# Clustered attention and two expert layers on one core: first pair's cluster steps by head, centroids loaded by ScalarE, more declared waits, new listed priorities

## The chip, the cores and the metric

The kernel runs on one core of a Trainium2 chip. The metric is the device time of one execution in microseconds (us), as the median of several runs. Beside it stands one profiled execution, with a trace of every instruction on TensorE (PE, with its weight loads PEld), VectorE (DVE), ScalarE (ACT), GpSimd (POOL) and SyncE (SP), which issues most DMAs.

## The reference, cut to what matters

```python
def _attn_ref(q, k, v, centroids):            # (2, 8, 768, 64) each; centroids (8, 16, 64)
    q_assign = argmax(einsum('bhsd,hcd->bhsc', q_n, c_n))   # all normalised
    k_assign = argmax(einsum('bhsd,hcd->bhsc', k_n, c_n))
    mask = q_assign[..., :, None] == k_assign[..., None, :]
    scores = where(mask, scale * q @ k.T, -1e9)
    attn = softmax(scores)
    return attn @ v
...
def _moe_ref(x, w_in, w_out):                 # 1536 x 512, 512 x 2048, 2048 x 512
    h = x @ w_in
    return (h * sigmoid(1.702 * h)) @ w_out
...
def _moe2_ref(x, w_in, w_out, g_ln):          # 512 x 1024, 1024 x 512
    ln = layer_norm(h * softmax(h)) * g_ln    # h = x @ w_in
    return ln @ w_out
```

Attention feeds the first layer, the first layer the second. In the attention a token sees only the tokens of its own cluster.

## The kernel before, in words

**The attention.** Sixteen heads (two batches of eight) go through in eight pairs. For a pair p, `operands_of` loads q and k, turns them on TensorE (`turn`, L557), splits each into a high and a low half (`turn_high` on ScalarE, L564 and L566; `turn_low` on VectorE, L573) and multiplies them with the centroids (`logits`, L587). The logits are copied (`logits_copy`, L594), turned back (`logits_turn`, L600), and five VectorE steps make a one-hot row of the first largest cluster: `cluster_max`, `cluster_equal`, `cluster_weigh`, `cluster_first` and `cluster_halves` (L608 to L631). The one-hot rows are turned (`cluster_turn`, L639), copied to SBUF (`cluster_copy`, L661) and moved by DMA into the operands `OP1` (`place_cluster`, through `move`, L664). For head 0 alone TensorE writes the rows without a DMA (`cluster_rows`, L647, and `cluster_place`, L655 and L657). Pairs 0 and 1 share the start: the whole of pair 0's loads and pair 1's come first.

For a head u, `peaks_of` multiplies nine tiles to find the largest score of each row (`peak`, L936, tile `sm`; `peak_max`, a VectorE reduction, L947, into `nma`). From these come the minimum (`peak_all`, L959), its transpose (`peak_turn`, L963) and a row of the operands (`peak_rows`, L968 on VectorE for the first two heads; later `peak_copy` and a DMA). `scores_of` multiplies the nine score tiles again with that row included (`score`, L995 and L996, tile `st` or `tx`), takes the exponential (L1004, ScalarE), casts to 16 bits (`cast`, L1009), takes the rest (`rest`, L1013, on GpSimd, or on VectorE where the tile "stays" in PSUM) and multiplies with the values (`value`, L1028 to L1032, tile `av`).

**Scales.** `values` bounds the values; `power_from` (L147 to L155) makes powers of two out of sums; `x_power` (L852, L853) makes the scale of the attention's result out of the longest value row (`longest`, L839). VectorE runs it.

**The layers.** `rest_of_layer` multiplies the first layer's hidden units (`Hidden.products`, L1200, tile `hps`), the second half of the program, from about 220 us, the rest (L1517, L1551, L1696). A second planner orders that half, and the diff does not touch it.

**What sets the order.** Every operation is a task of `Plan`, with a cost per engine, a due time, the tasks it comes after (`after`), and the buffer it takes or frees. `Plan.order` walks through a model of the engines, and at each step gives an engine the task with the lowest due time among those that are possible about then. A task with `shared=True` waits on VectorE until the modelled GpSimd is free. The order that comes out is the order in which each engine's queue is filled, and it is fixed when the kernel is built. Semaphores keep the true dependences. `SHIFTS` is a table of task numbers whose due times are shifted by fixed amounts. Where TensorE's modelled queue is empty in the first 36 us, dummy products are put in (L1339, tile `idle`).

```python
t = min((t["due"] - (STAY if eng == "PE" and t["kind"] and kind else 0.0), t["id"], i) for i, (a, t) in enumerate(at) if a <= first + ...)
```

Of the kernel before, what the change touches and what calls it, by code (L numbers as in the profile page):

```python
# [21 lines left out]
def kernel(  # L22
# [51 lines left out]
    XDUE = 30  # L74
    VDUE = 15
    VLC = dict(DVE=0.93, POOL=2.55)
    SOON = 10
    WAHEAD = -80
# [15 lines left out]
    ADUE = 4.5  # L94
    AVC = 0.373
    STAY = 0.0
# [71 lines left out]
    class Weight:  # L168
# [319 lines left out]
    t0 = add(dict(SP=(0.47, 0.18)), -70, lambda t: nc.sync.dma_start(cen, centroids.rearrange("h c d -> (h c) d")))  # L488
# [114 lines left out]
    def groups(t):  # L603
        return t.rearrange("p (g o) -> p g o", o=1).to_broadcast([P, G, C])

    def cluster_max(t, p):
        mxs[p] = oh_p.tile([P, G], F32, tag="mx", name="mx")
        nc.vector.tensor_reduce(out=mxs[p], in_=t["tile"], op=ALU.max, axis=AX.X)  # L608

    def cluster_equal(t, p):  # L610


        eqs[p] = t["tile"]
        nc.vector.tensor_tensor(out=eqs[p], in0=t["tile"], in1=groups(mxs[p]), op=ALU.is_equal)

    def cluster_weigh(p):
        nc.vector.tensor_tensor(
            out=eqs[p], in0=eqs[p], in1=first.rearrange("p (o c) -> p o c", o=1).to_broadcast([P, G, C]), op=ALU.mult
        )

    def cluster_first(p):
        m2s[p] = oh_p.tile([P, G], F32, tag="m2", name="m2")
        nc.vector.tensor_reduce(out=m2s[p], in_=eqs[p], op=ALU.max, axis=AX.X)

    def cluster_halves(p):

        eq = eqs.pop(p).rearrange("p (j s i) c -> p s j i c", s=2, i=2)
        m2 = m2s.pop(p).rearrange("p (j s i o) -> p s j i o", s=2, i=2, o=1)
        ohs[p] = oh_p.tile([P, NJ, 2, 2, C], BF16, tag="oh", name="oh")
        for s, op in enumerate((ALU.is_lt, ALU.is_equal)):  # L630
            nc.vector.tensor_tensor(  # L631
                out=ohs[p][:, :, s], in0=eq[:, s], in1=m2[:, s].to_broadcast([P, NJ, 2, C]), op=op
            )
# [54 lines left out]

    def operands_of(p):
# [4 lines left out]
        for s in range(2):  # L694
# [7 lines left out]
            for i in range(2):  # L702
                T["L", p, s, i] = add(
                    dict(SP=(0.65, 1.0)), n0 + LDUE if p > 1 else -62, lambda t, s=s, i=i: load(p, s, i),
                    after=[at("TT", p - 1, 2)] + late(True) if p > 1 else [],
                )
        for e in range(3):
# [4 lines left out]
                after=[a, at("ST", 2 * (p - NHL) + 1, NU - 1)],  # L712
# [5 lines left out]
        for n in range(2):  # L718
# [10 lines left out]
        b = add(dict(DVE=0.47), n0 + 18, lambda t, a=a: cluster_max(a, p), after=[a, at("C4", p - 1)])  # L729
        b = add(dict(DVE=0.47), n0 + 18, lambda t, a=a: cluster_equal(a, p), after=[b])  # L730
        b = add(dict(DVE=0.47), n0 + 19, lambda t: cluster_weigh(p), after=[b])
        b = add(dict(DVE=0.47), n0 + 20, lambda t: cluster_first(p), after=[b])
        b = T["C4", p] = add(
            dict(DVE=0.54), n0 + 21, lambda t: cluster_halves(p), after=[b, at("TO", p - 1)], frees=a
        )
        for e in range(0 if p else 3):
            a = add(dict(PE=0.3), n0 + 21, lambda t, e=e: cluster_rows(t, e), after=[b], take="ex")
# [4 lines left out]
        a = T["TO", p] = add(dict(PE=0.45), n0 + 22, lambda t: cluster_turn(t, p), after=[b], take="ex")  # L742
# [4 lines left out]
        for i in range(2):  # L747
            u = 2 * (p - NS) + i
            before = [at("ST", u, NU - 1), at("SM", u, NU - 1)]
# [58 lines left out]
    def values():  # L808
# [50 lines left out]
        add(dict(DVE=1.1), XDUE, lambda t, a=a: x_power(a), after=[a, scales["v"]], frees=a)  # L859
        T["VF"] = add(dict(DVE=0.1), 8, lambda t: factor(), after=list(scales.values()))  # L860
# [211 lines left out]
    def peaks_of(u):  # L1072
# [21 lines left out]
        if u >= RWS:  # L1094
# [9 lines left out]
            T["RW", u] = add(dict(SP=(0.65, 0.05)), n0 + NU - 18, lambda t: peak_row(u), after=[a, at("ST", u - 4, NU - 1)])  # L1104
# [3 lines left out]
    def scores_of(u):  # L1108
# [45 lines left out]
        if i:  # L1154
            a = add(
                dict(ACT=0.73, DVE=0.5), n + 12, lambda t: x_high(t, p), after=[T["N", u], T["N", u - 1], at("TX", p - 1, 0)],
# [3 lines left out]
            for e, c in enumerate((a, b)):  # L1160
                T["TX", p, e] = add(
                    dict(SP=(1.25, 0.9)), n + 20, lambda t, e=e: x_turn(p, e),
# [144 lines left out]
    for p in range(NH // 2):  # L1307
# [743 lines left out]
```

## Time and profile before

| what | value |
|---|---|
| median of 3 runs | 591.79 us (591.66 to 591.95) |
| the profiled execution | 592.09 us |
| its span in the trace | 590.3 us |
| PE busy | 579.9 us (98%) |
| DVE busy | 454.1 us (77%) |
| ACT busy | 418.5 us (71%) |
| POOL busy | 278.7 us (47%) |
| chain that ended last | PE 92%, DVE 4%, ACT 1%, DMA 1%, issue 1% |

The profiled execution lies 0.30 us above the median; 1.8 us of it lie outside the span. Busy shares are means over stages with different limits: the attention (to about 220 us) is one stage, the layers are another. Times in the trace count from the start of the span.

### The profile page before, as it was taken

Reading aid. Unit: us, or ns where it says so; the run is one execution under the profiler, and the core shown is the slowest. Engines: PE = TensorE matmul, PEld = TensorE weight load, DVE = VectorE, ACT = ScalarE, POOL = GpSimd, SP = SyncE. Lnnn points to the kernel's source line nnn. Section 1 sums busy time; section 2 is a strip of 40 time slices with the busy share of each in tenths; the row PEclk is TensorE's granted clock in tenths of the full one; section 3 lists DMA queues with packets and bytes.
Section 4 is the critical chain, followed back from the end, with each engine's and each line's share of the span. In section 5 each row is a group of like instructions: output and inputs, shape, how many; then the busy total and the mean of one; then the engine's idle time right before and its main releaser. Section 6 shows DMA issues by size and latency. Waiting matters only on the chain.

```text
span 590.3 us, 12602 instructions
## 1 busy us (share of the span) xinstructions
PE 579.9 (98%) x4790; PEld 387.1 (66%) x4790; DVE 454.1 (77%) x924; ACT 418.5 (71%) x799; POOL 278.7 (47%) x262
## 2 busy tenths in 40 slices
PE   7999999999999999999999999999999999999997
PEld 5788888888888876666666666666655664444444
DVE  5999998898999997899888731984996427996820
ACT  5799989988999978788878356563647614647831
POOL 7469979977778764344682037802100300133100
PEclk9999999999999999999999999999999999999999
DMA  8976969797773026443650530320000530043571
GB/s 206 229 190 151 218 136 204 154 193 154 152 146 63 17 64 203 146 140 145 213 180 1 179 109 0 108 72 0 1 2 1 72 72 0 37 72 82 113 146 53
DMA packets 79732, 65.28 MB, mean 111 GB/s; under 512 B 63620, under 2 KB 66520, under 8 KB 79672
## 3 DMA queue, kind: packets, MB, share of 16 engines
q1 hardware_dynamic: 79672, 64.49, 45.2%
q8 instruction: 37, 0.61, 0.4%
q14 instruction: 23, 0.19, 0.1%
HBM read 34.64 MB, written 3.15 MB: 64 GB/s over the span
## 4 chain that ended last, share of the span: by engine, by line
PE 92%; DVE 4%; ACT 1%; DMA 1%; issue 1%; SPq 0%; DVEq 0%; ACTq 0%
PE bank L1696 20%; PE hps L1200 16%; PE bank L1517 16%; PE st L995 6%; PE sm L936 5%; PE bank L1200 5%; PE bank L1551 5%; PE st L996 5%; PE av L1028 3%; PE av L1032 3%; PE ex L587 3%; PE av L1031 3%; PE ex L557 1%; DVE nma L947 1%; DMA reg<-in_q_dram 1%
## 5 line engine op out<-in xcount | busy, mean ns | idle before, releaser
L1013 POOL TENSOR_TENSOR ph<-p,ph 128x512 f16<-128x512 f32 x116 | 135.8, 1194 | 31.9 <-ACT ph L1009 17.8
L1200 PEld LDWEIGHTS <-reg 128*128 128x128 f16 x768 | 75.1, 98 | 48.9
L947 DVE TENSOR_REDUCE nma<-sm 128x1 f32<-128x512 f32 (+1 forms) x144 | 95.7, 681 | 5.7 <-PE sm L936 5.3
L1517 PE MATMUL bank<-g,reg 128*128 128x384 f16 x576 | 94.4, 326 | 0.0
L1200 PE MATMUL hps<-xT,reg 128*128 128x384 f16 x576 | 94.3, 326 | 0.0
L1517 PEld LDWEIGHTS <-reg 128*128 128x128 f16 x576 | 56.4, 98 | 37.2
L1215 POOL TENSOR_SCALAR g<-g,scl 128x384 f32<-128x384 f32 x40 | 37.4, 935 | 82.5 <-ACT g L1210 78.6
L1696 PE MATMUL bank<-reg,g 128*128 128x512 f16 (+1 forms) x366 | 75.0, 365 | 0.0
L1696 PEld LDWEIGHTS <-g 128*128 128x128 f16 x438 | 42.9, 98 | 46.8
L1004 ACT ACTIVATE p<-st 128x512 f32<-128x512 f32 x115 | 67.8, 601 | 7.8 <-PE st L996 5.0
L1009 ACT CAST ph<-p 128x512 f16<-128x512 f32 x107 | 64.2, 623 | 1.9 <-PE av L1032 1.2
L996 PE MATMUL st<-OP 97*128 97x512 f32 (+3 forms) x196 | 62.9, 336 | 0.0
L1028 PE MATMUL av<-vh,ph 128*128 128x65 f16 x576 | 62.2, 194 | 0.0
L1032 PE MATMUL av<-vh,ph 128*128 128x65 f16 x576 | 61.3, 195 | 0.7 <-DVE ph L1013 0.7
L1031 PE MATMUL av<-vh,ph 128*128 128x64 f16 x576 | 61.4, 193 | 0.0
L1028 PEld LDWEIGHTS <-ph 128*128 128x128 f16 x576 | 52.7, 99 | 11.0 <-issue 9.3
L936 PE MATMUL sm<-OP 80*128 80x512 f32 (+1 forms) x192 | 56.0, 359 | 1.7 <-DVE nma L947 1.4
L1032 PEld LDWEIGHTS <-ph 128*128 128x128 f16 x576 | 53.7, 97 | 1.0 <-DVE ph L1013 0.9
L1031 PEld LDWEIGHTS <-ph 128*128 128x128 f16 x576 | 53.8, 97 | 0.1
L1899 POOL TENSOR_TENSOR small<-small,mhalf 128x2 f32<-128x2 f32 (+1 forms) x7 | 4.6, 655 | 81.0 <-DVE small L1895 81.0
L1216 POOL TENSOR_TENSOR g<-g,g 128x384 f16<-128x384 f32 x40 | 40.4, 1010 | 3.3
L936 PEld LDWEIGHTS sm<-OP 80*128 80x128 f32 x192 | 33.8, 190 | 8.4 <-DVE nma L947 2.8
(255 smaller groups left out, 1188.3 us busy)
## 6 DMA issues: line engine op xcount, KB each, us to landing
OP<-hl SPq DMA_DIRECT2D x32, 384.0 KB, 5.3
raw<-in_moe_w_in_dram SPq DMA_DIRECT2D x24, 512.0 KB, 3.5
raw<-in_moe_w_out_dram SPq DMA_DIRECT2D x24, 512.0 KB, 4.2
xT<-in_v_dram SPq DMA_DIRECT2D x8, 384.0 KB
hl<-hl SPq DMA_DIRECT2D x8, 384.0 KB, 5.6
raw<-in_k_dram SPq DMA_DIRECT2D x12, 192.0 KB, 3.4
raw<-in_q_dram SPq DMA_DIRECT2D x12, 192.0 KB, 5.3
OP<-oht SPq DMA_DIRECT2D x30, 48.0 KB, 2.2
```

The source lines that it names most:

```text
L936: nc.tensor.matmul(t["tile"][:, at], Q1[0:KM, j * P:(j + 1) * P], K1[0:KM, cs], start=True, stop=True)
L947: nc.vector.tensor_reduce(out=out, in_=src, op=ALU.max, axis=AX.X, negate=True)
L996: nc.tensor.matmul(t["tile"][:, at], K1[0:n, ks], Q1[0:n, cs], start=False, stop=True)
L1004: nc.scalar.activation(p32s[u, m], t["tile"], AF.Exp, scale=SCALE)
L1009: e(phs[u, m][:, 0], p32s[u, m])
L1013: e.tensor_tensor(out=phs[u, m][:, 1], in0=p32s.pop((u, m)), in1=phs[u, m][:, 0], op=ALU.subtract)
L1028: nc.tensor.matmul(av[:, i, :], ph[:, 0, qs], vh[:, u, kt, D:], start=(m == 0 and kt == 0 and i == 0), stop=False,)
L1031: nc.tensor.matmul(av[:, i, 0:D], ph[:, 0, qs], vh[:, u, kt, 0:D], start=False, stop=False)
L1032: nc.tensor.matmul(av[:, i, :], ph[:, 1, qs], vh[:, u, kt, D:], start=False, stop=(m == NU - 1 and kt == NJ - 1 and i == NJ - 1),)
L1200: nc.tensor.matmul(self.ps, w1.at(c, m, e), xT[:, x, c, n * TB:(n + 1) * TB], start=(c == 0 and e == x), stop=(c == ND - 1 and e == 1),)
L1517: nc.tensor.matmul(out_, wo.at(f, c, e), lp["g", n][:, x, f, :], start=(f == 0 and e == x), stop=(f == NF - 1 and e == 1),)
L1696: nc.tensor.matmul(out_, data, weight, start=start and i == 0, stop=stop and i == n - 1)
```

## The change

- The task that loads the centroids is issued by ScalarE and no longer by SP.
- For pair 0 alone, each of the five cluster steps is split in two, one task for each head of the pair (`of_head`); the rows of head 0 (`cluster_rows`) come after head 0's steps alone, the transposes (`cluster_turn`) after both.
- `x_power` and `factor` are declared as sharing the port with GpSimd (`shared=True`), and the due time of the chain that ends in `x_power` moves from 30 to 90 (`XDUE`).
- More waits are declared to the planner: all nine tiles of a head in place of the last one (`all_of`), both transposing DMAs of a pair before its successor's `x_high`, and an earlier `TT` before a load.
- Numbers of the planner are set anew (`SOON`, `WAHEAD`, `ADUE`, `STAY`, a cost), and the table `SHIFTS` is replaced.

```diff
-    XDUE = 30
+    XDUE = 90
-    SOON = 10
-    WAHEAD = -80
+    SOON = 6
+    WAHEAD = -40
-    ADUE = 4.5
+    ADUE = 5
-    STAY = 0.0
+    STAY = 2.0
...
-    t0 = add(dict(SP=(0.47, 0.18)), -70, lambda t: nc.sync.dma_start(cen, centroids.rearrange("h c d -> (h c) d")))
+    t0 = add(dict(SP=(0.0, 0.18)), -70, lambda t: nc.scalar.dma_start(cen, centroids.rearrange("h c d -> (h c) d")))
...
+    def of_head(t, i):
+        if i is None:
+            return t
+        if len(t.shape) == 2:
+            return t.rearrange("p (g i) -> p i g", i=2)[:, i]
+        return t.rearrange("p (g i) c -> p i g c", i=2)[:, i]
+
+    def cluster_max(t, p, i):
+        if p not in mxs:
+            mxs[p] = oh_p.tile([P, G], F32, tag="mx", name="mx")
+        nc.vector.tensor_reduce(out=of_head(mxs[p], i), in_=of_head(t["tile"], i), op=ALU.max, axis=AX.X)
...
+        for i in (None,) if p else (0, 1):
+            c, d = (0.47, 0) if p else (0.28, i)
+            b = add(dict(DVE=c), n0 + d + 18, lambda t, y=y, i=i: cluster_max(y, p, i), after=[y, at("C4", p - 1)])
...
+            T.setdefault(("C4", p), b)
+        ones_of = [T["C4", p], b]
+        T["C4", p] = b
         for e in range(0 if p else 3):
-            a = add(dict(PE=0.3), n0 + 21, lambda t, e=e: cluster_rows(t, e), after=[b], take="ex")
+            a = add(dict(PE=0.3), n0 + 21, lambda t, e=e: cluster_rows(t, e), after=[ones_of[0]], take="ex")
...
-            before = [at("ST", u, NU - 1), at("SM", u, NU - 1)]
+            before = all_of("ST", u) + all_of("SM", u)
...
-        add(dict(DVE=1.1), XDUE, lambda t, a=a: x_power(a), after=[a, scales["v"]], frees=a)
-        T["VF"] = add(dict(DVE=0.1), 8, lambda t: factor(), after=list(scales.values()))
+        add(dict(DVE=1.1), XDUE, lambda t, a=a: x_power(a), after=[a, scales["v"]], frees=a, shared=True)
+        T["VF"] = add(dict(DVE=0.1), 8, lambda t: factor(), after=list(scales.values()), shared=True)
...
-                dict(ACT=0.73, DVE=0.5), n + 12, lambda t: x_high(t, p), after=[T["N", u], T["N", u - 1], at("TX", p - 1, 0)],
+                dict(ACT=0.73, DVE=0.5), n + 12, lambda t: x_high(t, p), after=[T["N", u], T["N", u - 1], at("TX", p - 1, 0), at("TX", p - 1, 1)],
...
     SHIFTS = {
-        38: -3, 65: -7, 119: 2.5, 144: -2.5, 146: 6.5, 200: -1, 208: -1.5, 227: -2, 233: 1, 265: 2, 270: -0.5,
+        18: 5, 31: -4.5, 36: -4, 119: -1, 135: 3, 139: -13.5, 142: -5.5, 178: 2.5, 282: -3.5, 288: 9.5, 333: -3,
...
```

The order that the planner makes differs on every engine. At the start, SP's queue loses the centroids' load and takes the loads of pair 1 (`in_k`, `in_q`, 128x6x64 each) in another sequence; the difference, with the lines of before marked - and those of the change marked +:

```order
-L488 DMA tmp<-in_centroids_dram 128x64
 L542 DMA reg_105<-in_k_dram 128x2x384
 L542 DMA reg_105<-in_q_dram 128x2x384
-L533 DMA reg_105<-in_q_dram 128x6x64
 L533 DMA reg_105<-in_k_dram 128x6x64 x2
-L533 DMA reg_105<-in_q_dram 128x6x64
```

(The two `in_q` lines of pair 1 follow as one line, x2.) The loads of pair 0's k and q now stand first. VectorE's cluster steps of pair 0, before:

```order
L608 TENSOR_REDUCE mx<-ex 128x24
L614 TENSOR_TENSOR ex<-ex,mx 128x384
L617 TENSOR_TENSOR ex<-ex,first 128x384
L623 TENSOR_REDUCE m_281<-ex 128x24
L631 TENSOR_TENSOR oh<-ex,m_281 128x6x32 x2
L573 TENSOR_TENSOR hl<-ex,hl 128x256 x2
```

and now:

```order
L615 TENSOR_REDUCE mx<-ex 128x12 x2
L623 TENSOR_TENSOR ex<-ex,mx 128x12x16
L629 TENSOR_TENSOR ex<-ex,first 128x12x16
L623 TENSOR_TENSOR ex<-ex,mx 128x12x16
L636 TENSOR_REDUCE m_282<-ex 128x12
L629 TENSOR_TENSOR ex<-ex,first 128x12x16
L650 TENSOR_TENSOR oh<-ex,m_282 128x6x16 x2
L636 TENSOR_REDUCE m_282<-ex 128x12
L650 TENSOR_TENSOR oh<-ex,m_282 128x6x16 x2
```

The steps of the two heads alternate, and head 0's one-hot rows (the first `oh` line) come after nine instructions in place of six; the `hl` line of pair 1 that followed now stands ahead of the steps. A little later, in head 0's peaks, the reduction of a fourth tile stands between a minimum (L959 before, L988 now) and the row made of it (L968, L997 now); before, nothing did.

VectorE around `x_power`, before, in pair 3's time (`longest` had been reduced some 30 lines earlier):

```order
L617 TENSOR_TENSOR ex<-ex,first 128x384
L947 TENSOR_REDUCE nma<-sm 128x1
L147 TENSOR_REDUCE scl<-ex 128x1
L149 TENSOR_SCALAR scl<-scl 128x1
L150 TENSOR_SCALAR scl<-scl 128x1
L151 TENSOR_SCALAR scl<-scl 128x1
L155 TENSOR_SCALAR scl<-scl 128x1 x2
L852 TENSOR_TENSOR scl<-scl 128x1
L853 TENSOR_TENSOR scl<-scl 128x1
L947 TENSOR_REDUCE nma<-sm 128x2
```

and now, in pair 7's time:

```order
L976 TENSOR_REDUCE nma<-sm 128x2
L976 TENSOR_REDUCE nma<-sm 128x1
L147 TENSOR_REDUCE scl<-ex 128x1
L149 TENSOR_SCALAR scl<-scl 128x1
L150 TENSOR_SCALAR scl<-scl 128x1
L151 TENSOR_SCALAR scl<-scl 128x1
L155 TENSOR_SCALAR scl<-scl 128x1 x2
L881 TENSOR_TENSOR scl<-scl 128x1
L882 TENSOR_TENSOR scl<-scl 128x1
L976 TENSOR_REDUCE nma<-sm 128x1
L1072 TENSOR_SCALAR ri<-av 128x6
```

The chain moved some 150 instructions of VectorE towards the end of the attention, to the operands of the last pair.

VectorE at the end of the attention, the casts and rests of the last head's last tiles, with buffer numbers; before:

```order
L1009 CAST ph_4590<-st_4551 128x512
L205 SCALAR_TENSOR_TENSOR reg1_105<-raw_2901,reg1_105 128x512
L1013 TENSOR_TENSOR ph_4590<-st_4551,ph_4590 128x512
L1009 CAST ph_4630<-st_4592 128x512
L196 TENSOR_SCALAR reg1_105<-raw_3345 128x512
L1013 TENSOR_TENSOR ph_4630<-st_4592,ph_4630 128x512
```

and now:

```order
L1038 CAST ph_4588<-st_4549 128x512
L201 SCALAR_TENSOR_TENSOR reg1_105<-raw_3246,reg1_105 128x512
L1042 TENSOR_TENSOR ph_4588<-st_4549,ph_4588 128x512
L1042 TENSOR_TENSOR ph_4625<-st_4590,ph_4625 128x512
L205 SCALAR_TENSOR_TENSOR reg1_105<-raw_3246,reg1_105 128x512
```

The last tile's cast went to ScalarE, and no step of a weight (L196) stands before its rest. On TensorE the twelve value products of that tile now stand behind the first twelve products of the first layer, whose PSUM bank is the one that this rest reads.

## Rows read from the trace of the kernel before

**Rows 1.** Busy time of each engine by stretch, whole core.
```profile
core 0: us, PE busy (x) PEld busy (x) DVE busy (x) ACT busy (x) POOL busy (x), PEclk, DMA share, GB/s
0.00:20.00 20.00, 16.09 (x119) 12.70 (x120) 13.09 (x55) 10.28 (x20) 10.57 (x16) 1.00 0.90 218
20.00:30.00 10.00, 9.07 (x60) 7.33 (x59) 9.24 (x22) 8.89 (x20) 7.03 (x6) 1.00 0.95 218
30.00:80.00 50.00, 48.60 (x599) 41.04 (x598) 48.02 (x109) 46.70 (x88) 41.60 (x35) 1.00 0.77 177
80.00:150.00 70.00, 70.00 (x905) 60.40 (x904) 62.31 (x124) 63.91 (x123) 60.93 (x52) 1.00 0.85 172
150.00:220.00 70.00, 69.03 (x1008) 58.85 (x1005) 65.37 (x132) 64.59 (x123) 53.71 (x45) 1.00 0.42 88
220.00:585.00 365.00, 365.00 (x2098) 205.12 (x2097) 256.12 (x487) 223.20 (x427) 104.84 (x110) 1.00 0.31 86
```

**Rows 2.** Waits of PE: line, who was waited for, us in total, times, longest.
```profile
PE sm L936 <- DVE nma L947: 1.4, 2, 1.0
...
PE av L1032 <- DVE ph L1013: 0.7, 2, 0.5
...
PE sm L936 <- DMA OP<-oht: 0.3, 1, 0.3
```

**Rows 3.** Timeline of SP's queue, first loads (start, us, line, tiles).
```profile
0.73 0.39 SPq L488 DMA_DIRECT2D tmp<-in_centroids_dram  x1
1.18 0.42 SPq L542 DMA_DIRECT2D reg<-in_k_dram  x1
1.64 0.47 SPq L542 DMA_DIRECT2D reg<-in_q_dram  x1
```

**Rows 4.** Timeline of ACT, then of PE, at the start.
```profile
2.49 0.26 ACT L489 ACTIVATE tmp<-tmp 128x64 f32<-128x64 f32 x1 [0.48 <-DMA tmp<-in_centroids_dram]
...
6.26 0.93 ACT L549 COPY raw<-reg 128x512 f32<-128x512 f32 x2 [0.66 <-DMA reg<-in_q_dram]
...
9.14 1.28 PE L587 MATMUL ex<-hl,cb 128*128 128x384 f32 x6 [0.56 <-DVE hl L573]
```

**Rows 5.** Timeline of DVE at the start.
```profile
6.26 0.93 DVE L483 CAST cb<-ex 64x64 fp32r<-64x64 f32 x4 [0.88 <-PE ex L475]
7.70 1.95 DVE L573 TENSOR_TENSOR hl<-ex,hl 128x512 fp32r<-128x512 f32 x4 [0.51 <-ACT hl L564]
...
13.81 0.55 DVE L608 TENSOR_REDUCE mx<-ex 128x24 f32<-128x384 f32 x1
...
16.19 0.62 DVE L631 TENSOR_TENSOR oh<-ex,m 128x192 bf16<-128x192 f32 x2
...
22.06 0.42 DVE L968 TENSOR_TENSOR OP<-tx,ident 6x256 fp32r<-6x256 f32 x1 [0.50 <-PE tx L963]
```

**Rows 6.** One line's instructions, L631: duration ns min/median/max, first and last start.
```profile
L631 DVE TENSOR_TENSOR oh<-ex,m x16: 344/348/357, 16.2 to 176.6; 128x192 bf16<-128x192 f32 x16
```

**Rows 7.** Timelines of POOL, DVE and PE around 72 us.
```profile
69.30 5.63 POOL L1013 TENSOR_TENSOR ph<-p,ph 128x512 f16<-128x512 f32 x5
...
71.75 0.96 DVE L852 TENSOR_TENSOR scl<-scl 128x1 f32<-128x1 f32 x1
72.64 1.20 DVE L853 TENSOR_TENSOR scl<-scl 128x1 f32<-128x1 f32 x1
...
74.50 0.50 PE L936 MATMUL sm<-OP 80*128 80x256 f32 x2 [0.96 <-DVE nma L947]
```

**Rows 8.** Timeline of PE at 184.75 us, head 14's first peak.
```profile
184.75 0.48 PE L936 MATMUL sm<-OP 80*128 80x512 f32 x1 [0.29 <-DMA OP<-oht]
```

**Rows 9.** Timelines of DVE and PE at the end of the attention.
```profile
218.58 0.69 DVE L1013 TENSOR_TENSOR ph<-st,ph 128x512 f16<-128x512 f32 x1
...
219.32 0.20 PE L1032 MATMUL av<-vh,ph 128*128 128x65 f16 x1 [0.53 <-DVE ph L1013]
```

**Rows 10.** DMA issues to 32 us: pair 1's q, KB each, us to landing.
```profile
reg<-in_q_dram SPq DMA_DIRECT2D x2, 192.0 KB, 5.0
```

More of the change, by code (lines that the diff above doesn't have):

```diff
@@ L601, in logits_turn @@
         t["tile"] = x[:, 0:HT].rearrange("p (g c) -> p g c", c=C)
[L603 to L610, printed above, removed]
+    def of_head(t, i):
[4 more added lines that the diff above has]
+        return t.rearrange("p (g i) c -> p i g c", i=2)[:, i]
@@ L619, in cluster_weigh @@
         )
[L621 to L629, printed above, removed]
-        for s, op in enumerate((ALU.is_lt, ALU.is_equal)):
-            nc.vector.tensor_tensor(
-                out=ohs[p][:, :, s], in0=eq[:, s], in1=m2[:, s].to_broadcast([P, NJ, 2, C]), op=op
-            )
+    def cluster_weigh(p, i):
+        x = of_head(eqs[p], i)
+        nc.vector.tensor_tensor(
+            out=x, in0=x, in1=first.rearrange("p (o c) -> p o c", o=1).to_broadcast([P, x.shape[1], C]), op=ALU.mult
+        )
@@ new lines, in cluster_first, with cluster_halves @@
+    def cluster_first(p, i):
+        if p not in m2s:
+            m2s[p] = oh_p.tile([P, G], F32, tag="m2", name="m2")
+        nc.vector.tensor_reduce(out=of_head(m2s[p], i), in_=of_head(eqs[p], i), op=ALU.max, axis=AX.X)
+    def cluster_halves(p, i):
+        eq = eqs[p].rearrange("p (j s i) c -> p s i j c", s=2, i=2)
+        m2 = m2s[p].rearrange("p (j s i o) -> p s i j o", s=2, i=2, o=1)
+        if p not in ohs:
+            ohs[p] = oh_p.tile([P, NJ, 2, 2, C], BF16, tag="oh", name="oh")
+        oh = ohs[p].rearrange("p j s i c -> p s i j c")
+        for s, op in enumerate((ALU.is_lt, ALU.is_equal)):
+            if i is None:
+                o, x, m = (y.rearrange("p i j c -> p j i c") for y in (oh[:, s], eq[:, s], m2[:, s]))
+                nc.vector.tensor_tensor(out=o, in0=x, in1=m.to_broadcast([P, NJ, 2, C]), op=op)
+            else:
+                nc.vector.tensor_tensor(
+                    out=oh[:, s, i], in0=eq[:, s, i], in1=m2[:, s, i].to_broadcast([P, NJ, C]), op=op
+                )
@@ L687, in late, with all_of @@
         return [T["PC", 0, 0, 1]] if x else []
+    def all_of(name, u):
+        return [at(name, u, m) for m in range(NU)]
     def operands_of(p):
@@ L704, in operands_of @@
                     dict(SP=(0.65, 1.0)), n0 + LDUE if p > 1 else -62, lambda t, s=s, i=i: load(p, s, i),
-                    after=[at("TT", p - 1, 2)] + late(True) if p > 1 else [],
+                    after=[at("TT", p - 1, s), at("TT", p - 1, 2)] + late(True) if p > 1 else [],
                 )
@@ L711, in operands_of @@
                 dict(ACT=0.48), n0 + 3 * e, lambda t, e=e, a=a: turn_high(a, p, e),
-                after=[a, at("ST", 2 * (p - NHL) + 1, NU - 1)],
+                after=[a] + all_of("ST", 2 * (p - NHL) + 1),
             )
@@ L741, in operands_of @@
             )
-        a = T["TO", p] = add(dict(PE=0.45), n0 + 22, lambda t: cluster_turn(t, p), after=[b], take="ex")
+        a = T["TO", p] = add(dict(PE=0.45), n0 + 22, lambda t: cluster_turn(t, p), after=ones_of, take="ex")
         b = add(
@@ L1103, in peaks_of @@
             )
-            T["RW", u] = add(dict(SP=(0.65, 0.05)), n0 + NU - 18, lambda t: peak_row(u), after=[a, at("ST", u - 4, NU - 1)])
+            T["RW", u] = add(dict(SP=(0.65, 0.05)), n0 + NU - 18, lambda t: peak_row(u), after=[a] + all_of("ST", u - 4))
     todo, held = [], []
```

24 lines of the change are left out of this document (13 added, 11 removed), and 14 rows, old and new, of the table SHIFTS.

## The prediction

> **What bounds the kernel now.** I read the stretches first [rows 1]. From 220 to 585 us TensorE is busy for 365.00 of 365.00 us at full granted clock, and the diff does not touch that half: it can only begin earlier or later. So the change is worth what it does to the moment at which the attention ends, near 220 us. Up to there TensorE is idle for 3.91 us of the first 20, 0.93 of the next 10, 1.40 between 30 and 80, nothing between 80 and 150, and 0.97 between 150 and 220. The first 20 us are worse than that, because dummy products count as busy. Between 30 and 80 us VectorE is busy for 48.02 of 50 us, so TensorE's idle time there is VectorE's lateness. Second I read who TensorE waits for [rows 2]: the reductions of peaks, the rests of the last tiles, one DMA of one-hot rows. So I add up what the change does at the start, and at the few places where TensorE waits by name.
>
> **The sum, part by part**, against the profiled execution (592.09 us, 0.30 above the median); the result is set against the median of 591.79.
>
> *The centroids' load by ScalarE.* SP issues it from 0.73, k at 1.18, q at 1.64 [rows 3]. Without it k and q move up by 0.45 us. The q copy is what ScalarE waits for at 6.26, by name [rows 4], and the chain goes on through TensorE's transposes, ScalarE's casts, VectorE's lows at 7.70 [rows 5] to the logits at 9.14 [rows 4]. The other branch, the centroids, ends at 7.19 on VectorE (0.93 after 6.26) [rows 5]: 0.51 us of cover, and 0.06 after the lows have moved up by 0.45. ScalarE's first square waits 0.48 us for the centroids anyway [rows 4], which covers the issue in front of its table load. Bounds: -0.45, if nothing new is late, and 0, if the centroids come later by that much. I take **-0.4**, near the bound that the named wait speaks for.
>
> *Cluster steps by head.* Before, the steps start at 13.81 and the last pair of instructions ends at 16.81: 3.00 us, and the starts lie (16.19-13.81)/4 = 0.595 apart, each step waiting for the one before [rows 5]. The trace does not show steps of 192 elements in this place, but L631 is of that size: 0.348 us for one [rows 6], 0.62 for two that do not depend on each other [rows 5], so the second starts 0.62-0.348 = 0.27 after the first. In the new order head 0's result stands behind nine instructions: seven of 192 elements, of which one follows directly on the step it needs. That is 6 x 0.27 + one at 0.348+0.04 + the closing pair. The pair has 96 elements each: at most 0.62, at least half of it, 0.31. Sum 2.32 to 2.63, against 3.00. If no two steps overlapped it would be 7 x 0.348 + 0.62 = 3.06. So the bounds are +0.06 and -0.68. I take **-0.4**, the careful end of the overlapping case, since the new order alternates the two heads. Head 1's steps run while TensorE writes head 0's rows.
>
> [...]
>
> *Head 0's peaks.* VectorE idles 0.50 us before the row of the first peaks, for TensorE's transpose [rows 5]. In the new order the reduction of the fourth tile stands in that gap. Bounds -0.5 and 0; **-0.3**, since the first row itself comes a little later and the scores of head 0 with it.
>
> *The two scale products.* L852 and L853 are 128x1, yet take 0.96 and 1.20 us [rows 7]. GpSimd runs five rests back to back from 69.30 to 74.93, 1.126 each: it changes from one to the next at 72.68 and 73.81, and the two products end at 72.71 and 73.84. They wait for the end of a GpSimd instruction. The next reduction on VectorE is late, and TensorE idles 0.96 us at 74.50 [rows 7]: the longest wait in [rows 2]. The chain moves to the last pair's operands, after 150 us, where VectorE is busy for 65.37 of 70 [rows 1]. At the old place I take **-1.0** (0.96 of idle and the restart); bounds 0, if another wait moves in at once, and -1.1. At the new place GpSimd is busy for 53.71 of 70 [rows 1], so the two products may wait again, up to 1.2 each. What is queued behind them on VectorE is one reduction, the normalisation of a head and a second reduction; TensorE waits for those only through PSUM buffers, with six tiles of value products, score tiles and the next transposes queued in front. **+0.2**, bounds 0 and +1.0 (the old wait again).
>
> *Head 14's rows.* At 184.75 TensorE waits 0.29 us for the one-hot rows of the last pair [rows 8]. Between that pair's one-hot transposes and head 14's first peak TensorE's queue holds 60 value products, 5 score tiles and 1 peak tile before, and 84, 7 and 3 in the new order. **-0.3**, bounds -0.3 and 0.
>
> *The end of the attention.* TensorE waits 0.53 us at 219.32 for the last tile's rest, which starts at 218.58 behind a weight step [rows 9]. Now the cast is ScalarE's and the rest follows the rest before it. TensorE's first layer product, which stands ahead of the last values, needs the bank that this rest reads, so the wait is moved to it, not gone; but the rest comes about one VectorE step earlier. **-0.5**, bounds 0 and -0.7.
>
> *A new order's own waits.* From 30 to 220 us TensorE idles 1.40+0.97 = 2.37 us [rows 1], and the three kinds in [rows 2] make 2.4 of it, in five waits, 0.47 on average. I have taken the ones that I can name; a new order will have some of its own. I take one of mean size, **+0.5**; bounds -0.4 (the one unnamed wait goes too) and +2 (two of the longest, 1.0, come in). The declared waits cost no instruction, and the other moved loads lie in queues that TensorE nowhere waits for by name.
>
> Sum: -0.4 - 0.4 - 0.3 - 1.0 + 0.2 - 0.3 - 0.5 + 0.5 = **-2.2**, so 591.79 - 2.2 = **589.6 us**. A difference of 0.2% (1.2 us) is about what a measurement can tell from none.
>
> **Rivals.**
> [...]
> *Given back.* Only the start moves (-1.1), and the waits further on are replaced: the scale products meet GpSimd again and TensorE idles 1.0 at the new place, the last rows and the end change nothing, one wait of mean size comes in. -0.4-0.4-0.3-1.0+1.0+0.5 = -0.6: 591.2. For it: VectorE's 48.02 of 50 between 30 and 80, which leaves little room to catch up. Against it: 2.1 us of that load are the two products.
> *Slower: the second pair's transposes ahead of the logits.* In the new order the first four transposes of pair 1 stand on TensorE before pair 0's logits; before, they stood behind the first half of them. If pair 1's k has not landed, logits and all that follows wait. Its second half is now SP's fourth load, so issued from about 2.1 us (three issues of up to 0.47 after 0.73 [rows 3]); pair 1's q landed 5.0 us after its issue [rows 10], which makes 7.1, or somewhat more where the queue is full, and the logits would start at 8.7. From a landing there on each us costs one, and the kernel is slower by 1.2 only from 8.7+2.2+1.2 = 12.1 on: a time of 593.0. The row speaks against it.
>
> **How the numbers follow.** Forecast 0.56, fixed cost 0.15, given back 0.22, slower 0.07. Faster by over 0.2% (below 590.6): nearly all of the first, most of the second, a quarter of the third, 0.72. Slower (above 593.0): the last and the far end of new waits, 0.08. Between: 0.20. The range: low with the start's, the peaks' and the end's better bounds, -0.45-0.68-0.5-1.1-0.3-0.7 and the waits at +0.1, together -3.6: 588.2, taken to 588.0; high at the third case with a little of the new waits' bound, 591.3. That leaves about 2 in 10 outside.
>
> **What would show it.** Right: k's issue at about 0.73 and the q copies near 5.8; head 0's one-hot rows about 2.6 us after the first maximum; first peaks near 17.5 in place of 18.35; no wait of TensorE for a reduction near 74; the attention's end some 2 us earlier, and every later stretch as long as before. Wrong: waits of TensorE between 30 and 220 us that add up to more than the old 2.37; two products near 1 us long after 150 us with idle time on TensorE right behind; the logits waiting for a DMA.

## The result, and the profile after

The changed kernel takes **598.99 us** (median of five, 598.34 to 600.65) against 591.79: ratio 1.0116, interval 1.0093 to 1.0139, so about 6.9 us slower; 589.6 was predicted. Its profiled execution took 598.34 us, with a span of 596.5 against 590.3.

Busy time by stretch, after (compare [rows 1]; of its last row two parts are shown):

```profile
0.00:20.00 20.00, 15.63 (x108) 12.60 (x109) 13.08 (x57) 9.86 (x19) 10.59 (x16) 1.00 0.81 200
20.00:30.00 10.00, 9.59 (x58) 7.52 (x57) 9.67 (x25) 7.77 (x17) 4.81 (x4) 1.00 0.82 210
30.00:80.00 50.00, 47.57 (x566) 39.48 (x566) 44.76 (x98) 46.25 (x85) 42.79 (x36) 1.00 0.78 176
150.00:220.00 70.00, 69.93 (x988) 59.90 (x987) 65.02 (x137) 67.05 (x129) 54.39 (x46) 1.00 0.43 85
280.00:325.00 45.00, 41.63 (x253) 24.62 (x252) 35.02 (x67) 33.63 (x72) 23.50 (x25) 1.00 0.44 141
325.00:585.00 260.00, 260.00 (x1442) 140.88 (x1441) 173.54 (x320) 142.41 (x257) 55.23 (x63) 1.00 0.25 61
```

From 280 to 325 us TensorE is idle for 3.37 us, where [rows 1] had none; from 80 to 150 and from 220 to 280, not shown, for 0.08 and 0.23. Who it waits for, after (compare [rows 2]):

```profile
PE ex L475 <- DVE chl L467: 1.3, 1, 1.3
PE tot L141 <- ACT junk L218: 1.2, 1, 1.2
PE hps L1229 <- DVE g L1247: 0.9, 1, 0.9
PE ex L557 <- DMA raw<-in_q_dram: 0.7, 1, 0.7
PE ex L557 <- ACT ph L1038: 0.7, 1, 0.7
PE ex L557 <- DVE nma L976: 0.6, 1, 0.6
PE hps L1229 <- ACT g L1236: 0.5, 1, 0.5
```

The reductions' wait of 1.0 and the wait for `oht` are gone. New are the centroids (`chl`), pair loads, and three waits in the first layer. Those stand in TensorE's timeline, first after, then before:

```profile
283.46 25.57 PE L1229 MATMUL hps<-xT,reg 128*128 128x384 f16 x156 [0.88 <-DVE g L1247]
310.23 0.40 PE L141 MATMUL tot<-wss,ones 128*128 128x16 f32 x2 [1.20 <-ACT junk L218]
311.17 7.96 PE L1229 MATMUL hps<-xT,reg 128*128 128x384 f16 x48 [0.54 <-ACT g L1236]
318.96 1.14 PE L1576 MATMUL bank<-g,reg 128*128 128x384 f16 x6
```

```profile
307.80 0.29 PE L141 MATMUL tot<-wss,ones 128*128 128x16 f32 x2
307.94 6.01 PE L1200 MATMUL hps<-xT,reg 128*128 128x384 f16 x36
313.79 2.44 PE L1551 MATMUL bank<-g,reg 128*128 128x384 f16 x14
```

L141 with 16 columns sums the squares of `w_out` (L218); without that sum the weight has no scale, and without the scale the layer's second product (`bank`) cannot start. The first layer's first block starts at 221.19 (before 219.65: +1.5), its second product at 318.96 (before 313.79: +5.2), and the end is 6.2 later. So 1.5 us were lost up to this first block (0.9 of it already at the first peak, 19.26 against 18.35), 3.6 from there to the second product, and about 1 right behind, in two more waits. The twelve value products that stood ahead of the first block now stand behind it, so the second block is 1.9 us late (223.51 against 221.59): like for like, 1.9 us were lost in the attention and 3.3 in the layer.

ScalarE's last square of `w_out`, after and before:

```profile
309.45 0.63 ACT L218 ACTIVATE junk<-reg 128x512 bf16<-128x512 f32 x1 [0.59 <-DVE reg L205]
```

```profile
305.61 0.63 ACT L218 ACTIVATE junk<-reg 128x512 bf16<-128x512 f32 x1
```

Before, the squares ended at 306.24 and TensorE came to the sum at 307.80: 1.5 us of slack, behind a stretch in which TensorE was busy without a gap. Now they end at 310.08, and the sum stands one block of twelve products earlier (528 products of `hps` ahead of it, not 540).

Where the conversion becomes late: SP's weight loads around the attention's end, after and before.

```profile
221.76 0.94 SPq L185 DMA_DIRECT2D raw<-in_moe_w_in_dram  x2
226.48 2.55 SPq L1097 DMA_TRANSPOSE xT<-xh  x2
229.13 16.94 SPq L185 DMA_DIRECT2D raw<-in_moe_w_in_dram  x6
```

```profile
217.16 3.79 SPq L185 DMA_DIRECT2D raw<-in_moe_w_in_dram  x2
222.79 2.66 SPq L1068 DMA_TRANSPOSE xT<-xh  x2
225.56 21.51 SPq L185 DMA_DIRECT2D raw<-in_moe_w_in_dram  x8
```

The first two loads wait for a buffer that the narrowing step L205 frees; it now stands behind the last rests (221.05, before 216.45). The rest queue behind two transposing DMAs, which wait for ScalarE's cast of the attention's last result, and that cast now stands behind the first gate and its table load, and its input behind the last value products. ScalarE after, then before:

```profile
223.26 1.28 ACT L1236 ACT_TABLE_LOAD   x1
224.56 0.56 ACT L1236 ACTIVATE hps<-hps,scl 128x384 f32<-128x384 f32 x1
225.15 0.58 ACT L1239 ACTIVATE g<-hps,scl 128x384 f16<-128x384 f32 x1
225.63 0.82 ACT L1087 CAST xh<-xs 128x768 f16<-128x768 f32 x1
```

```profile
221.93 0.83 ACT L1058 CAST xh<-xs 128x768 f16<-128x768 f32 x1 [0.53 <-DVE xs L1051]
223.43 1.28 ACT L1207 ACT_TABLE_LOAD   x1 [0.66 <-DVE scl L1174]
```

The cast starts 3.70 us later. For 2.8 of that its input (`xs`, a VectorE step) was not ready: it ends at 224.71, before at 221.90, since the last value products stand behind the first block. The gate ahead of it held it for the last 0.9.

One correction to the words ahead of the prediction: the first layer's blocks and the weights' conversion are tasks of the same plan as the attention (`rest_of_layer`), so `WAHEAD`, `SHIFTS` and every other number of the plan set their order too. A second planner orders only what comes from that layer's second product (`bank`) on.

### The profile page after: what moved, and what is told of

It reads as the page before. It is cut to its first block, busy times and chain, and to the rows that moved or that the text cites. A ratio compares the mean times of both kernels' runs of the same rounds, so it can differ in the third digit from the quotient of the medians.

```text
span 596.5 us, 12615 instructions
## 1 busy us (share of the span) xinstructions
PE 582.4 (98%) x4783; PEld 387.5 (65%) x4783; DVE 455.6 (76%) x928; ACT 421.9 (71%) x802; POOL 279.9 (47%) x259
## 4 chain that ended last, share of the span: by engine, by line
PE 76%; DVE 12%; DMA 5%; ACT 5%; issue 1%; POOL 0%; SPq 0%; ACTq 0%; DVEq 0%
PE bank L1721 20%; PE bank L1542 16%; PE st L1024 6%; PE sm L965 5%; PE bank L1229 5%; PE st L1025 5%; PE bank L1576 5%; PE av L1057 3%; PE av L1061 3%; PE av L1060 3%; PE ex L587 2%; DVE reg L201 2%; DMA raw<-in_moe_w_out_dram 2%; DVE reg L205 2%; DVE nma L976 2%; PE ex L557 2%
## 5 line engine op out<-in xcount | busy, mean ns | idle before, releaser
L976 DVE TENSOR_REDUCE nma<-sm 128x1 f32<-128x512 f32 x144 | 95.4, 681 | 6.7 <-PE sm L965 6.2
L1244 POOL TENSOR_SCALAR g<-g,scl 128x384 f32<-128x384 f32 x40 | 40.9, 1023 | 81.9 <-ACT g L1239 68.6
L965 PE MATMUL sm<-OP 80*128 80x512 f32 (+1 forms) x192 | 57.4, 362 | 0.3 <-DVE nma L976 0.2
L1025 PEld LDWEIGHTS st<-OP 97*128 97x128 f32 (+1 forms) x196 | 37.4, 191 | 2.3 <-issue 0.2
```

Of the source, the lines that this page charges most:

```text
L965: nc.tensor.matmul(t["tile"][:, at], Q1[0:KM, j * P:(j + 1) * P], K1[0:KM, cs], start=True, stop=True)
L976: nc.vector.tensor_reduce(out=out, in_=src, op=ALU.max, axis=AX.X, negate=True)
L1025: nc.tensor.matmul(t["tile"][:, at], K1[0:n, ks], Q1[0:n, cs], start=False, stop=True)
```

## The experiments

Ratios are to the kernel before; us are (ratio - 1) x 591.7. Two theories. *Late weights*: the changed listing makes the conversion of the weights late. *Order of the layer* or *no slack*: the layer's own listing, or whatever is late ahead of it, makes the waits.

**Undoing single entries in the changed kernel (e1 to e4).** e1 puts one number back; e2 to e4 move tasks in the list that the planner made:

```diff
-    WAHEAD = -40
+    WAHEAD = -80
```

```diff
     order = plan.order()
+
+    def ahead(x, y):
+        t = next(t for t in order if t["id"] == x)
+        order[:] = [s for s in order if s is not t]
+        order.insert(next(n for n, s in enumerate(order) if s["id"] == y), t)
+
+    for x, y in ((1447, 1635), (1448, 1636), (1449, 1636), (1450, 1636), (1451, 1636)):
+        ahead(x, y)
```

(e2: the last values ahead of the first block, the cast ahead of the first gate. e3 has the pairs (1458, 1427), (1465, 1434) and (1466 to 1468 and 1485, 1448): L205 and a load earlier, the seventh tile's steps and one more load ahead of the last normalisation. e4 has both lists.)

> The changed kernel with WAHEAD back at -80; the order of every engine is the changed kernel's up to about 300 us, and only the weights' steps and the products behind that are listed otherwise. Theory late weights: the conversion of the weights already starts some 4.7 us late at the attention's end (the L205 steps run at 221.05 and 221.65 where they ran at 216.45 and 219.90 before, the third pair of loads is issued at 229.13 and not at 225.56), and that is untouched here: 599 us, within 1 us of the changed kernel, waits of TensorE between 280 and 325 us still about 4. Rival order of the layer: the number WAHEAD has put the first layer's own tasks in a worse order: the waits at 310 to 321 us go, 595 us.

> The changed kernel, but the last twelve value products stand ahead of the first layer's first block on TensorE again, and the cast of the last pair's result (x_high) ahead of the first gate on ScalarE. Theory late weights: the two transposing DMAs, which stand ahead of the weights' loads on SP and wait for that cast, are issued near 224.5 in place of 226.48, the loads behind them near 227 in place of 229.13, and half of the waits at 280 to 325 us goes: 597 us. Rival order of the layer: nothing depends on when these loads come; the first gate comes about 1 us later: 599 to 600 us.

> The changed kernel, but the last step of the fifth weight tile (L205) stands on VectorE some eight instructions earlier, the load that takes its buffer follows at once, the seventh tile's three steps stand ahead of the last normalisation, and one more load stands ahead of the two transposing DMAs on SP. Theory late weights: the load at 221.76 moves to about 214, the conversion runs 4 to 5 us earlier from there on, the waits of TensorE at 310 to 321 us go: 595 us, and the attention's end moves by less than 0.7 us. Rival order of the layer: 599 us, with the same waits at 280 to 325 us.

> The moves of the last two kernels together. Theory late weights: the gains don't add up, since the waits at 280 to 325 us can go only once: 594 to 595 us. Rival order of the layer: 599 to 600 us.

Measured: e1 598.24 (1.0105, 1.0089 to 1.0120), e2 598.56 (1.0119, 1.0096 to 1.0141), e3 600.74 (1.0145, 1.0128 to 1.0162), e4 602.83 (1.0187, 1.0171 to 1.0202). No undo helps by more than the intervals, and two cost. e1 fits its first theory by the time alone, e2 lies between its two, e3 and e4 lie above every range that I had given. e1's waits moved on: there the sum stands later, and TensorE waits 1.97 us for the converted `w_out` itself:

```profile
314.03 0.29 PE L141 MATMUL tot<-wss,ones 128*128 128x16 f32 x2
318.25 0.50 PE L1576 MATMUL bank<-g,reg 128*128 128x384 f16 x2 [1.97 <-ACT reg L239]
```

In e3 the first load was issued at 217.30 and not at 214, behind two transposes in SP's queue (issued from 209.08 to 212.86); the seventh tile was done early, the ninth as late as ever (237.1), because its steps stand behind the layer's own on VectorE, and TensorE waited 1.0 us for the last rest behind the moved step. So these four did not decide between the theories; late weights as I had put it (one early start repairs it) was wrong.

**Whole listings exchanged (e5, e6, e9, e10).** The list is cut, and the rest stands in the other kernel's order, with its engines and PSUM banks:

```diff
+    REST = (
...
+    )
+    named = {t["id"]: t for t in order}
+    order = order[:1410] + [named[i] for i in REST]
+    for i, x in ENGINES.items():
+        named[i]["eng"] = x
+    for i, x in BANKS.items():
+        named[i]["buffer"] = x
```

> The changed kernel up to the last 15 us of the attention; from there on every engine's instructions stand in the order of the kernel before (PSUM banks and engines as there). Theory late weights: 5 of the 7 us lost lie in the listing of the attention's end and the first layer, which decides when the weights' conversion starts and how it is woven between the layer's steps; with the old listing the waits at 280 to 325 us go (below 1 us) and what is left is the attention's own lateness of 1.5 us: 593.3 us, 592.5 to 594.5. Rival no slack: those waits come from whatever is late ahead of them, in any listing: they stay, 597 to 599 us.

> The converse: the kernel before up to the last 15 us of the attention, and from there on every engine's instructions in the order of the changed kernel. Theory late weights: the weights start late here too and the waits at 280 to 325 us appear: 596 to 597.5 us. Rival no slack: the attention ends as early as before, so no new wait: 592 to 593 us.

> The kernel before up to the first few blocks of the first layer (some 320 operations are left, the first weight loads behind the transposing DMAs are listed as before); from there on the changed kernel's order. Theory late start: the conversion starts as early as before, so the late squares of w_out do not arise: 592 to 593 us. Theory weave: the way in which the changed order threads the weights' steps and the sum over w_out's squares (L141, 16 columns, one block earlier on TensorE) between the layer's blocks costs the time, whenever the conversion starts: 596 to 597.5 us, with TensorE waiting for L218 ahead of that sum.

> The kernel before with only the stretch from the last 15 us of the attention to the first few blocks of the first layer in the changed order, and the order of before again from there on. Theory late start: the loads behind the transposing DMAs are issued 2 to 3 us later, and the conversion stays late to the end: 595 to 597 us. Theory weave: 592 to 593 us.

Measured: e5 594.99 (1.0055, 1.0040 to 1.0070: +3.3), e6 597.67 (1.0099, 1.0086 to 1.0113: +5.9). From 280 to 325 us, e5 and then e6:

```profile
280.00:325.00 45.00, 45.00 (x280) 27.18 (x279) 38.15 (x73) 37.12 (x77) 24.91 (x24) 1.00 0.43 141
```

```profile
280.00:325.00 45.00, 41.32 (x251) 24.33 (x249) 34.55 (x67) 34.02 (x72) 23.64 (x24) 1.00 0.41 141
```

With the old listing from the attention's end on, no idle time, although the first layer began 2.4 us late (222.04 against 219.65); with the new one 3.68 us, although it began within 0.3 us of before (219.94). That settles the place: most of the loss belongs to the listing behind the attention, 5.9 us where it is put behind the old attention and 3.6 (6.9 - 3.3) where it is taken from behind the new one. The two parts, 3.3 and 5.9, make more than 6.9, so they are not independent; and at e5's joint TensorE waits 0.5 us for the attention's last rest, where the changed kernel waits 0.17.

e9 596.26 (1.0070, 1.0055 to 1.0086: +4.1) and e10 596.00 (1.0074, 1.0057 to 1.0090: +4.4): each half alone costs most of it, and together they cost 5.9, not 8.5. In e9 TensorE waits at the sum (1.18 and 0.54 us), in e10 mostly for `g` (1.4 us in two waits); e13 to e15 make these waits one by one. That both halves come down to one late conversion fits this and is not shown by itself.

**Single entries put into the kernel before (e13, e14, e15, e17).** The helper of e2 with other pairs: e13 has the first line, e14 the second, e15 the third (the fifth tile's L205, the load behind it, and the seventh tile's steps with theirs), e17 all of them.

```diff
+    for x, y in ((1620, 1806),):
...
+    for x, y in ((1630, 1442), (1631, 1446), (1632, 1446)):
...
+    for x, y in ((1453, 1443), (1460, 1443), (1454, 1459), (1461, 1467), (1462, 1468), (1463, 1641), (1464, 1643), (1480, 1643)):
```

> The kernel before with one operation moved: the sum over w_out's squares (L141, 16 columns) stands one block of twelve products earlier on TensorE. Theory weave by the sum alone: TensorE waits there and pays about 4 us, as with the changed order from the layer on: 595 to 596 us. Rival late conversion: the squares end near 306.3 us here, 0.5 us after TensorE gets to the sum, and the following 48 products make up for it: 591.8 to 592.6 us.

> The kernel before, but the first layer's first block stands ahead of the last twelve value products on TensorE, and the first gate and its table load ahead of the cast of the last pair's result (x_high) on ScalarE. If the transposing DMAs and the weights' loads behind them on SP make the conversion late: the transposes are issued 2 to 3.5 us later than 222.79, the third pair of loads later than 225.56 by as much, and the kernel is slower by 1.5 to 3 us: 593.3 to 594.8 us. Rival: the loads have slack: 591.5 to 592.3 us.

> The kernel before, but the last step of the fifth weight tile (L205) stands behind the last rest of the attention, the load into its buffer behind it, and the seventh tile's steps where they stand in the changed kernel. If the conversion's start is what costs: the load at 217.16 is issued near 220.5, everything behind it on that chain is 3 to 4 us later, slower by 2 to 4 us: 594 to 596 us. Rival: the conversion catches up: 591.5 to 592.5 us.

> The kernel before with the moves of e13, e14 and e15 together. If these three entries are what the changed listing costs from the attention's end on: they made 1.0, 1.8 and 1.7 us alone, so 595 to 597 us together, near the 597.7 us of the whole tail (e6). Rival: they are one late conversion seen three times, and together cost no more than the largest: 593.5 to 594.5 us.

Measured: e13 592.72 (1.0022, 1.0012 to 1.0032: +1.3), e14 593.46 (1.0032, 1.0016 to 1.0048: +1.9), e15 593.42 (1.0031, 1.0020 to 1.0042: +1.8), e17 596.43 (1.0068, 1.0045 to 1.0091: +4.0). e13 ends just above its rival's range, e14 and e17 in the range of the first theory, e15 between its two. In e14 the cast starts at 225.51 in place of 221.93; its input is only 0.45 us late, the rest is the gate and its table load. How this late cast reaches TensorE 50 us later: SP, VectorE, TensorE.

```profile
226.35 2.56 SPq L1068 DMA_TRANSPOSE xT<-xh  x2
229.02 21.12 SPq L185 DMA_DIRECT2D raw<-in_moe_w_in_dram  x8
```

```profile
269.39 0.86 DVE L196 TENSOR_SCALAR reg<-raw 128x512 uint32<-128x512 uint32 x1 [1.47 <-DMA raw<-in_moe_w_out_dram]
...
275.56 1.78 DVE L1218 SCALAR_TENSOR_TENSOR g<-hps,scl,g 128x384 f16<-128x384 f32 x3
```

```profile
276.23 6.01 PE L1200 MATMUL hps<-xT,reg 128*128 128x384 f16 x36 [1.08 <-DVE g L1218]
```

The loads come 3.5 us late, stay 2 to 3 us late, and VectorE stands 1.47 us idle for one; behind the weight's steps three steps of the layer (`g`) are queued, and TensorE waits for their PSUM banks. e15 does the same by the other road (load at 220.47, wait of 0.8 for `g`), and e13 by putting the sum where the squares are not yet done (wait of 0.67). The three named entries make 4.0 us together, of the 5.9 of the whole tail; the intervals (2.7 to 5.4 and 5.1 to 6.7 us) leave up to some 4 us to entries that were not tried one by one.

**The two scale products and the centroids (e7, e11, e16, e18).** e7 takes L852 and L853 out of `x_power` into a function that the first `scale_of` calls; e11 changes the issuing engine alone, e16 both; e18 undoes it in the changed kernel.

```diff
-            nc.vector.tensor_tensor(out=s, in0=s, in1=power_of["v"][1], op=ALU.mult)
-            nc.vector.tensor_tensor(out=i, in0=i, in1=power_of["v"][0], op=ALU.mult)
             power_of["x"] = s, i
...
         if c not in scales_of:
+            if not scales_of:
+                power_of["scaled"]()
```

```diff
-    t0 = add(dict(SP=(0.47, 0.18)), -70, lambda t: nc.sync.dma_start(cen, centroids.rearrange("h c d -> (h c) d")))
+    t0 = add(dict(SP=(0.47, 0.18)), -70, lambda t: nc.scalar.dma_start(cen, centroids.rearrange("h c d -> (h c) d")))
```

> The kernel before with nothing changed but the two scale products (L852, L853), which stand on VectorE ahead of the first layer's first scale, at about 224 us, and no longer at 72 us. Theory of my term: the wait of 0.96 us at 74.5 goes and nothing takes its place: 590.8 us, 590.5 to 591.0. Rival given back: another wait for VectorE between 72 and 90 us takes most of it: 591.4 to 591.9 us.

> The kernel before with nothing changed but the engine that issues the centroids' load (ScalarE); all orders stay. My term: k and q land up to 0.45 us earlier and the logits with them: 591.3 us. Rival late centroids: they land some 2.6 us after the issue where they took 1.7, ScalarE's first square starts 0.9 us later, and the centroids become the late branch ahead of the logits: 592.0 to 592.5 us.

> The kernel before with both the two scale products late and the centroids' load issued by ScalarE. If the load's engine is worth something by itself: 1 us less than the products alone, 589.5 us. Rival phase: with the load moved, the logits started at the same time (9.18 and 9.14 us) and what went was the same wait at 74.5 us, since the second product happened to miss GpSimd's next rest by 0.1 us; so the two gains don't add: 590.3 to 590.9 us.

> The changed kernel with nothing changed but the centroids' load, issued by SP again ahead of k; all orders stay. There the centroids' transposes stand first on TensorE, ahead of those of k and q. Theory late centroids: they land near 2.0 us, their transposes start near 5.0 in place of 5.96 us, the logits come some 0.4 to 0.7 us earlier, and the profile's first scores too: 598.3 us, with a profile whose logits start before 9.7 us. Rival: k and q, 0.45 us later again, take their place: logits at 10 us or later.

Measured: e7 590.61 (0.9981, 0.9964 to 0.9998: -1.1), e11 590.51 (0.9984, 0.9975 to 0.9994: -0.9), e16 590.60 (0.9986, 0.9975 to 0.9997: -0.8). The gains don't add. e11's logits start at 9.18 (before 9.14): q's copy moved up from 6.26 to 5.65, but the centroids' square moved back from 2.49 to 3.47. What e11 gained stands at 72 us on VectorE:

```profile
71.64 0.95 DVE L852 TENSOR_TENSOR scl<-scl 128x1 f32<-128x1 f32 x1
72.52 0.15 DVE L853 TENSOR_TENSOR scl<-scl 128x1 f32<-128x1 f32 x1
```

The second product took 0.15 us and not 1.20 [rows 7], and the wait at 74.5 did not arise: e11 lies below both its ranges for a reason that neither had. GpSimd's rests had moved by the same 0.11 us as the products (69.19 against 69.30), so the two stood to each other as before; what let the second product through is not shown. It is luck, and no merit of the load. e16, where the products are away from there, has nothing left to gain from the load. e7, e11 and e16, at 590.5 to 590.6 us, are the fastest kernels here, about 0.2% below the kernel before.

e18: 597.26 (1.0094, 1.0063 to 1.0126: +5.6). Its start, then the changed kernel's:

```profile
5.19 0.86 PE L475 MATMUL ex<-ident,chl 128*128 128x128 f32 x2 [0.54 <-DVE chl L467]
5.84 2.88 PE L557 MATMUL ex<-ident,raw 128*128 128x128 f32 x12
9.44 1.30 PE L587 MATMUL ex<-hl,cb 128*128 128x384 f32 x6
```

```profile
5.96 0.86 PE L475 MATMUL ex<-ident,chl 128*128 128x128 f32 x2 [1.31 <-DVE chl L467]
6.61 2.68 PE L557 MATMUL ex<-ident,raw 128*128 128x128 f32 x12
10.02 1.29 PE L587 MATMUL ex<-hl,cb 128*128 128x384 f32 x6
```

Logits 0.58 us earlier: in the changed listing the centroids stand first on TensorE, ahead of k and q, so there their load is the bound. The times' intervals overlap; the 0.58 is shown by the trace alone, where seven profiles with the changed start and ScalarE's load have their logits at 10.00 to 10.40.

**The split and the middle (e8, e12).** In e8 `of_head` returns the whole tile and the second head's five tasks return at once (*fixed cost*, here and in the prediction's chances, is the case in which the split steps don't overlap):

```diff
     def of_head(t, i):
-        if i is None:
-            return t
...
+        return t
...
     def cluster_max(t, p, i):
+        if i:
+            return
```

e12 is e5's edit with three pieces: before to 60 us, changed to the attention's end, before again.

> The changed kernel, but the five cluster steps of pair 0 are whole again: each stands where head 0's step stands now, and the second head's tasks emit nothing. My term (independent steps overlap): head 0's one-hot rows come later than in the changed kernel, and the time is 0.4 us more. Rival fixed cost: whole steps take 3.0 us as the split ones up to head 0's rows do (3.06), and VectorE has 0.8 us less to do: the first peaks come 0.5 to 0.8 us earlier, the time is 0.3 to 0.8 us less than the changed kernel's.

> The kernel before up to about 60 us, the changed order from there to the last 15 us of the attention (with the two scale products and the last pair's rows where the change has them), and the order of before to the end. If the parts of the change that held (no wait at 74.5, none at 184.75) are worth what they showed, 1.0 and 0.3 us, and the first layer keeps its old listing: 590.0 to 590.7 us. Rival: the joints make waits of their own, 591.5 to 592.5 us.

Measured: e8 597.52 (1.0095, 1.0079 to 1.0111), an interval that overlaps the changed kernel's, and its scores at 28.4 us come no earlier than the changed kernel's at 28.2, though its logits had started 0.25 us later (10.27 against 10.02): the split is worth nothing that shows. e12 591.50 (1.0006, 0.9996 to 1.0017): no change. The wait at 74.5 is gone there, and two of 0.4 us for VectorE at 62 and 65 us have come, right behind the joint at 60 us: the rival's joints.

## Why the prediction was wrong, point by point

**The step that failed** is the first paragraph's "the diff does not touch that half: it can only begin earlier or later", and with it "the other moved loads lie in queues that TensorE nowhere waits for by name". The diff did reorder the first layer and the conversion ahead of it; a second chain (loads, narrowing on VectorE, squares, sum, scale) ended only 1.5 us ahead of TensorE's need. "365.00 of 365.00" showed that nothing waited, not by how much. None of my rivals was this one; the one that ended slower (the logits) did not happen.

- *Centroids* (-0.4): the load by itself moved the logits by 0.04 us, well inside the spread of 8.56 to 9.43 that ten profiles with the start of before show: the bound "the centroids come later by that much" was the truth. In the changed listing +0.9 (10.02 against 9.14). A part of that can be the transposes of k and q, which took 0.22 us each there and 0.14 before (last section); the term did not have it.
- *Cluster steps* (-0.4): from the first maximum to the end of head 0's rows 3.06 us against 3.00. VectorE's steps after:

```profile
15.35 0.37 DVE L623 TENSOR_TENSOR ex<-ex,mx 128x192 f32<-128x192 f32 x1
15.75 0.37 DVE L629 TENSOR_TENSOR ex<-ex,first 128x192 f32<-128x192 f32 x1
16.15 0.37 DVE L623 TENSOR_TENSOR ex<-ex,mx 128x192 f32<-128x192 f32 x1
```

  They start 0.40 apart and last 0.37, the independent ones too. Here only two equal steps next to each other overlapped as [rows 5] had it (the two maxima take 0.61 together, the closing pair 0.42). So the bound without overlap held (3.06, *fixed cost* in the chances): term 0, which alone would have made the forecast 590.0.
- *Head 0's peaks* (-0.3): the gap is filled, but the row of the first peaks starts 0.79 us after its minimum where it was 0.65 (23.01 - 22.22; before 22.06 - 21.41): about 0.
- *Scale products* (-1.0 and +0.2): right. The wait is gone, L881 takes 0.76 us at 159.5 and TensorE does not wait there; by itself -1.1 (e7). The port that the change declares is the planner's model; what the trace shows is that both products ended 0.03 us behind the end of a GpSimd instruction [rows 7].
- *Head 14's rows* (-0.3): right, no wait at 184.75. *End of the attention* (-0.5): of the waits for the last rests one of 0.17 us is left in the list, where [rows 2] has 0.7: right. The words "not gone, moved" held too, but I did not ask what the moved blocks hold up on ScalarE and SP.
- *New waits* (+0.5): too small. From 28 to 61 us TensorE waits for `p`, `nma`, the exponential's cast and a pair's q; PE's busy time from 30 to 80 is 47.57, before 48.60. From 30 to 220 it idles 2.58 us, above the 2.37 that I had named as the sign of being wrong.

Up to the first layer's first block I predicted -2.2 and got +1.5; behind it 0 and got +4.7 (like for like +1.9 and +4.3).

## What to carry to other kernels

A stretch in which the bounding engine never waits has a slack that busy shares do not show: before you write "not touched", look up when each other chain that it needs (here the last square) ends and when it is needed (the sum), and check that the planner's table does not reach there. An entry's price is what stands behind it in the queues, engine after engine down to the bound: a cast moved behind a gate and its table load of 1.28 us (e14, with one block ahead of the last values) cost 1.9 us by way of SP's loads and VectorE, 50 us later. To price one entry of a new listing put it alone into the good kernel; undoing it in the bad one showed nothing here, since another entry made the same wait.

## What the runs showed of the hardware

The two waits around the sum (1.18 to 1.32 and 0.54 us) were followed by 48 products in 7.96 us in e6 and the changed kernel, and in 9.64 us in e3 and e9. The granted clock from 280 to 325 us is 1.00 in e6 and the changed kernel and 0.96 in e3 and e9. e9's timeline and its stretch:

```profile
307.51 0.40 PE L141 MATMUL tot<-wss,ones 128*128 128x16 f32 x2 [1.18 <-ACT junk L218]
308.45 9.64 PE L1200 MATMUL hps<-xT,reg 128*128 128x384 f16 x48 [0.54 <-ACT g L1207]
```

```profile
280.00:325.00 45.00, 43.27 (x256) 25.44 (x255) 34.73 (x64) 34.62 (x74) 23.83 (x24) 0.96 0.43 141
```

An estimate from these rows: 0.04 x 45 = 1.8 us of full clock were not granted, and the 48 products are 1.68 us longer. So waits of 1.7 us together were followed by a loss about as large in two of these four profiles; that the waits bring it about was not tried. The mean granted clock on record for each execution says how often: 0.997 in three of the five of the changed kernel (598.74, 599.64, 600.65 us) and 1.00 in two (598.34, 598.99), and never below 0.999 in 77 of the kernel before. What it costs in the median is not shown: in e9 the one execution at 0.997 (596.22) is no slower than two of the three at 1.00 (596.30, 596.33). A part of what e3 cost can be of this kind: from 220 to 280 us, the stretch with its wait of 1.0 us for a last rest, its granted clock is 0.97 too, an estimated 0.03 x 60 = 1.8 us of full clock.

Issuing the centroids' load (32 KB) from ScalarE took 0.42 us in e11, and its use came later, with k's load issued at the same time: the first square came 2.7 us after the issue (0.73 to 3.47), where it had been 1.8 (0.73 to 2.49 [rows 3, 4]). What made it later was not tried.

In the changed kernel twelve transposes took 2.68 us (0.22 each), behind TensorE's wait of 1.31 us for the centroids; before, eight of the same kind took 1.09 (0.14 each). In e18 twelve took 2.88 behind a wait of 0.54; in e11 four took 1.12 at 5.16 (0.28 each) and eight 1.04 at 6.58 (0.13). The stretches' rows give a granted clock of 1.00 for 6 to 9 us in the changed kernel and for 7 to 8 before, but the trace's record of the clock begins only at 9.06 us in the changed kernel, and at 5.08 before: what clock the slow twelve had is not shown. At 0.14 each they would take 1.0 us less, an estimate from these rows; how much of the logits' +0.9 that is was not tried.
